# First batch's keys loaded by groups, values loaded by heads into 96 partitions, in a polysketch attention + tanh-shrink kernel

## The chip, the cores and the metric

The kernel runs on one core of a Trainium2 chip. The time is device microseconds (us) of one execution. Before the change three timed runs gave 104.93, 105.68 and 105.86 us, a median of 105.68 us; the execution that was profiled took 104.86 us.

## The reference

Everything is float32. B = 4 batches, H = 4 heads, S = 1088 positions, D = 32, sketch rank r = 8; the second part sees 4 x 1088 = 4352 tokens of 128 features.

```python
def phi(x):                        # x: (B, H, S, D)
    a = einsum('rd,bhsd->bhsr', S1, x)
    b = einsum('rd,bhsd->bhsr', S2, x)
    return einsum('bhsi,bhsj->bhsij', a, b).reshape(..., 64)
q_p, k_p = phi(q), phi(k)
kv  = einsum('bhsf,bhsd->bhfd', k_p, v)      # sum over positions
z   = sum(k_p, axis=2)
num = einsum('bhsf,bhfd->bhsd', q_p, kv)
den = einsum('bhsf,bhf->bhs', q_p, z) + 1e-6
x   = (num / den) as (B*S, H*D) = (4352, 128)
h   = x @ w_in                               # w_in: (128, 2048)
out = (h - tanh(h)) @ w_out                  # w_out: (2048, 128)
```

Since h @ w_out = x @ (w_in @ w_out), the kernel computes `x @ (w_in @ w_out)` from a folded 128x128 matrix and adds `tanh(-h) @ w_out`.

## The kernel before, in words

**Layout.** A head's 1088 positions stand as 32 rows (j) of 34 consecutive positions (c). Keys and queries lie with head and j on the 128 partitions. Positions are cut into 9 tiles t; a tile holds 4 groups g of 32 rows. With c = 9g + t the values `vx` lie with (g, j) on 128 partitions and head, t, d behind each other; the last group has 7 tiles instead of 9.

**Attention, first batch.** `load_keys` brings `kraw`, `load_rows` the queries, `load_v` the values. DVE turns the keys by 32x32 blocks (`kT`, L595), PE projects them on the sketches (`kproj`, L604), DVE turns the result back (`kab`, L612). Two things follow. (1) `gram` (L620) sums the products of the two sketches of the keys; `zm` (L625), `ufold` (L629) and `uw` (L632) make from it a column block of `w4`, with which PE projects the queries (`qproj`, L774); DVE turns the result (`qab`, L782), computes the denominators (`dm`, `den`, `rden`, `qa`: L801 to L810) and the query products `qp` (L685). (2) The key products `wk` (L652, on POOL and DVE) are multiplied with the values on PE (`tiles`, L665), copied (`kvs`, L671), folded (L674) and copied again (`kvb`, L678). Both meet: PE turns `qp` (`qt0`, L700), ACT copies it (`qpB`, L707), PE multiplies it with `kvb` (`num0`, L716), and a copy gives the tokens `xT` in bf16 (L722). The copy `ka` (L641) puts one factor of `wk` into PSUM for DVE.

**The second part.** Tokens go in ten windows of 256 or 512. For each window and each of 16 hidden blocks `jb`, PE computes h (`L1`, L952), ACT its tanh (L956), PE the product with `w_out` (`L2`, L973). `casts` makes bf16 copies of the weights, `linear_turn` turns `w_in` (L886, L891) and `wfold` (L898) makes the folded matrix. The first window needs the tokens of tiles 0 and 1 of the first batch. Batches 1 to 3 do the same attention in larger pieces between the windows' matmuls. While PE has nothing to do at the start, matmuls on zeros (`fill`, L531 and L532) are put into its stream.

**What sets the order.** Each engine has its own stream, and each instruction stands where the table `ORDER` puts it: operation numbers by engine, written out. `PLACES` names the engine of operations that can run on more than one. A planner in the source (`schedule`) places the fills and the waits by cost estimates; on the chip an engine takes its instructions in this order and stands at the first whose data is missing. SP issues nearly all transfers, on one queue, also in the order of the table; a load of a later batch waits until few enough bytes are outstanding (`gated`).

**Order at the start of before.** SP: keys in three pieces, queries 0 to 511, four loads of values, two slices of `w_in`, the rest of the queries, two slices of `w_in`, four of `w_out`, then batch 1. DVE: `kT` in two pieces, `kab` for tiles 0-4, `qT` (which waits for the queries), `kab` for tiles 5-8, `qT`, `wk` 5, `zm`, `wk` 6, `uw`, `wk` 7 and 8, `qab`. PE, from `qproj`: all nine tiles of `tiles` in one stretch (it waits for the value loads, all on one semaphore), the fold, `qt0` of tiles 0 and 1 with two `turn`s between, `qt0` of tiles 2 and 3, three `num0`, a `turn`, and the first `L1`.

The loads of values, keys and the loop of the first products are in these functions:

Of the kernel before, what the change touches and what calls it, by code (L numbers as in the profile page):

```python
# [30 lines left out]
COLD = 6800  # L31
EARLY = 5000
CHUNK = 256
HEAD = 56
# [19 lines left out]
    ),  # L54
    "scalar": (
# [4 lines left out]
    ),  # L60
    "vector": (
# [5 lines left out]
    ),  # L67
    "gpsimd": (
        "4 15 17 16 2 3 25 5 20 19 21 77 75 18 76 102 103 107 104 24 106 146 148 23 238 237 22 243 247 360 359 361 370 366 502 "
        "503 504 509 513 "  # L70
    ),
    "sync": (
# [7 lines left out]
PLACES = {"qpB0.2": "scalar", "w_inT0": "scalar", "x0.2": "scalar", "cast_out1": "scalar", "qpB0.4": "scalar", "qpB0.6":  # L80
          "scalar", "x0.4": "scalar", "kvs3": "scalar", "w_inT1": "vector", "x0.1": "vector", "w_inT2":
          "vector", "x0.8": "vector", "kvw1": "vector", "kvs2": "vector", "cast_in3": "gpsimd", "cast_out2":
          "gpsimd"}
# [22 lines left out]
class Program:  # L106
# [13 lines left out]
    def op(self, eng, cost, fn, r=(), w=(), prio=0.0, sem=None, mode=None, name="", after=(), ni=2, two=False, alt=None):  # L120
# [5 lines left out]
        o.alt = alt  # L126
        for k in r:
# [17 lines left out]
        for k in r:  # L145
            if k not in w:
                self.readers.setdefault(k, []).append(o)
# [9 lines left out]
    def schedule(self):  # L157
# [21 lines left out]
        while left:  # L179
# [20 lines left out]
            if e == "tensor":  # L200
                if filling and o in self.fill_stops:
                    filling = False
                if filling and fills_from in order["vector"]:
                    free[e] = max(free[e], fills_from.at + fills_from.cost + 90, 990)
                    while True:
                        rate = 1.2 if free[e] < COLD else 2.4
                        wide = 512 if free[e] + 512 / rate + 60 <= o.at else 128
# [3 lines left out]
                        f = Op("tensor", long, self.filler[0 if wide == 512 else 2], 0, None, None, "fill")  # L211
# [12 lines left out]
                while passed // CHUNK > block:  # L224
                    block += 1
                    self.fetch.append((block, o.name, o.at, have[block] - o.at))
                    o.at = max(o.at, have[block])
                    have.append(o.at + (5800 if o.at < 24000 else 3500))
# [134 lines left out]
def bass_polysketch_attn__then__act_tanh_shrink_kernel(nc, q, k, v, S1, S2, moe_w_in, moe_w_out, out):  # L363
# [11 lines left out]
    def dve(n):  # L375
        return 75 + n / 0.96
# [58 lines left out]
    KG = 9 * 32  # L435

# [25 lines left out]
    def load_small():  # L462
        for i, src in enumerate((S1, S2)):
            o = load("scalar", 1024, ("s_raw",), "s", -1000, lambda e, i=i, src=src: e.dma_start(
                out=s_raw[8 * i:8 * i + 8, :], in_=src[:, :]), True)
            o.lag = 800 * i - 500
# [16 lines left out]
    def load_keys(prio):  # L483

        src = k[0].rearrange("h (j c) d -> (h j) (c d)", j=32)
        dst = kraw[0][:, :].rearrange("p (g f) -> p g f", f=KG)

        def runs(g0, g1, lo, hi):
            rows = src[:, KG * g0 + lo:KG * g0 + hi]
            rows = bass.AP(tensor=rows.tensor, offset=rows.offset, ap=[rows.ap[0], [KG, g1 - g0], rows.ap[1]])  # L490
            return lambda e: e.dma_start(out=dst[:, g0:g1, lo:hi], in_=rows)  # L491

        for x, (g0, g1, lo, hi) in enumerate(((0, 4, 0, 160), (0, 3, 160, 288), (3, 4, 160, 224))):
            size = 512 * (g1 - g0) * (hi - lo)
            o = load("sync", size, ("kraw0", min(x, 1)), f"k0{min(x, 1)}", prio, runs(g0, g1, lo, hi), x == 2, (350, 378, 100)[x])
            o.lag = (-200, 150, 150)[x]
            if x == 2:
                asked.append((o, size))

    def load_v(b, prio):  # L500
        i = b % 2
        src = v[b].rearrange("h (j c) d -> j h c d", j=32)
        for g in range(4):
            n = 9 if g < 3 else 7
            o = load("sync", 128 * 128 * n, ("vx", i), f"v{i}", prio, lambda e, g=g, n=n: e.dma_start(
                out=vx[i][32 * g:32 * g + 32, :, 0:n, :].rearrange("j h t d -> j h (t d)"),
                in_=src[:, :, 9 * g:9 * g + n, :].rearrange("j h t d -> j h (t d)")), True, 190 if b == 0 else 240)
            o.lag = 1500 if b == 1 else 0 if b else 300
        asked.append((o, 128 * 128 * 34))
# [19 lines left out]
    def constants():  # L529
        wzero = P.op("vector", 150, lambda e: e.memset(wz[:, :], 0.0), w=[("wz",)], prio=-2000, name="wz")  # L530
        P.filler = (lambda e: e.matmul(ps[:, FB, 0:512], wz[:, :], wz[:, None, :].to_broadcast([128, 4, 128]), start=True, stop=True), wzero,  # L531
                    lambda e: e.matmul(ps[:, FB, 0:128], wz[:, :], wz[:, :], start=True, stop=True))  # L532
# [26 lines left out]
    def sketch():  # L559
        def put(e):  # L560
            for h in range(H):
                e.matmul(ps[32 * h:32 * h + 32, 5, 0:32], s_raw[:, :],
                         ident[0:16, None, 0:16].to_broadcast([16, 2, 16]),
                         start=True, stop=True, tile_position=(0, 32 * h))
            for h in range(H):
                ins = e.matmul(ps[32 * h:32 * h + 32, 6, 64:96], e16[:, :, :].rearrange("p a b -> p (a b)")[:, 32 * h:32 * h + 32],
                               s_raw[:, :], start=True, stop=True, tile_position=(0, 32 * h))
            return ins

        P.op("tensor", 170, put, r=[("s_raw",), ("ident",), ("e16",)], w=[bank[5], bank[6]], prio=-3000, mode="32x32", name="psk", ni=32)  # L570
# [14 lines left out]
    def keys(b, T, kb, gb, gate=()):  # L585
# [3 lines left out]
        for x, (lo, hi) in enumerate(KCUT if b else KPART):  # L589
            if b:  # L590
                P.op("vector", dve(hi - lo), lambda e, lo=lo, hi=hi: e.transpose(  # L591
                    out=kT[:, lo:hi], in_=kraw[i][:, lo:hi]), r=cells("kraw", i, lo, min(hi, S)) + ([("kraw0", i, "z")] if x else []),
                    w=[("kT", x)], prio=T["kT"], after=gate, name=f"kT{b}{x}")
# [524 lines left out]
```

## Time and profile before

| what | value |
|---|---|
| timed runs, median of 3 | 105.68 us (104.93 to 105.86) |
| profiled execution, its own time | 104.86 us |
| span of that execution's trace | 102.6 us |
| outside the span | 2.26 us |
| PE busy | 96.7 us, 94% of the span |
| ACT busy | 79.2 us, 77% |
| DVE busy | 60.0 us, 58% |
| POOL busy | 34.1 us, 33% |
| first L1 matmul (L952) | 15.7 us after the span's start |
| bytes moved | 11.21 MB |

A busy PE is not a PE at its peak, since matmuls overlap in their pipeline: the sum of the single durations is larger than the time that passes. The view that says what sets the end is the chain of waits, which is followed back from the last instruction. Times below are from the start of the span unless they are durations.

### The profile page before, as it was taken

How to read it: one execution, taken by the hardware profiler on the slowest of the kernel's cores; microseconds unless marked ns; L12 is line 12 of the kernel's file. 1: busy time of each engine (PE TensorE's matmuls, PEld its weight loads, DVE VectorE, ACT ScalarE, POOL GpSimd, SP SyncE). 2: the span in 40 equal slices, each digit the busy share in tenths (PEclk: the TensorE clock that was granted, in tenths of full speed). 3: DMA queues.
4: the chain of work that ended last, by engine and by line, in shares of the span. 5: the costliest groups of instructions: out<-in, count | busy, mean ns of one | idle time of the engine just before them, and what ended most of it. 6: DMA issues, size and time to landing. Idle time of an engine off the chain costs nothing.

```text
span 102.6 us, 3008 instructions
## 1 busy us (share of the span) xinstructions
PE 96.7 (94%) x1278; PEld 52.2 (51%) x1278; DVE 60.0 (58%) x129; ACT 79.2 (77%) x110; POOL 34.1 (33%) x43
## 2 busy tenths in 40 slices
PE   6969989999999999999999999999999999999970
PEld 2336747884676543434555343644444434445760
DVE  0778975997999897699678437837840020020120
ACT  3431768978767956787998797999869999999970
POOL 5347345420956800973910079083000000000000
PEclk9999999999999999999999999999999999999999
DMA  2999999910079804870003544030013611016254
GB/s 46 292 216 309 388 382 270 205 30 6 13 170 235 264 12 135 205 228 0 6 0 58 112 85 93 8 47 0 0 19 55 92 26 19 0 27 98 45 80 93
DMA packets 24029, 11.21 MB, mean 109 GB/s; under 512 B 18000, under 2 KB 21200, under 8 KB 24016
## 3 DMA queue, kind: packets, MB, share of 16 engines
q1 hardware_dynamic: 23840, 10.95, 44.2%
q8 instruction: 10, 0.16, 0.7%
q10 hardware_dynamic: 176, 0.07, 0.2%
q14 instruction: 3, 0.02, 0.1%
HBM read 8.78 MB, written 2.23 MB: 107 GB/s over the span
## 4 chain that ended last, share of the span: by engine, by line
PE 86%; DVE 5%; DMA 4%; SPq 1%; issue 0%
PE ps L952 31%; PE ps L973 27%; PE ps L843 4%; DMA qraw<-in_q_dram 4%; PE ps L937 4%; PE ps L734 3%; PE ps L774 3%; PE ps L716 2%; PE ps L604 2%; PE ps L700 2%; PE ps L968 2%; DVE qp L685 2%; SPq L491 1%; PE ps L620 1%; PE ps L898 1%; PE ps L629 1%
## 5 line engine op out<-in xcount | busy, mean ns | idle before, releaser
L956 ACT ACTIVATE tt<-ps 128x1024 bf16<-128x1024 f32 (+1 forms) x70 | 66.2, 998 | 8.0 <-PE ps L952 7.7
L952 PE MATMUL ps<-xT,w_in 128*128 128x512 bf16 (+1 forms) x160 | 42.7, 351 | 0.0
L973 PE MATMUL ps<-tt,w_out 128*128 128x512 bf16 (+1 forms) x144 | 38.2, 356 | 0.0
L952 PEld LDWEIGHTS ps<-xT,w_in 128*128 128x128 bf16 x160 | 16.3, 115 | 14.7 <-ACT tt L956 3.7
L652 POOL TENSOR_TENSOR wk<-kab 128x768 f32<-128x768 f32 (+2 forms) x11 | 15.5, 1405 | 21.0 <-DVE kab L612 20.4
L973 PEld LDWEIGHTS ps<-tt,w_out 128*128 128x128 bf16 x144 | 14.1, 99 | 11.9 <-issue 0.9
L989 DVE STREAM_TRANSPOSE osb<-ps 128x512 f32<-128x512 f32 (+1 forms) x9 | 5.9, 657 | 20.5 <-PE ps L973 20.3
L820 POOL TENSOR_TENSOR qp<-qa,qab 128x768 f32<-128x768 f32 x6 | 10.6, 1768 | 7.2 <-DVE qa L810 6.9
L826 DVE STREAM_TRANSPOSE qpT<-qp 128x768 f32<-128x768 f32 x9 | 8.6, 964 | 3.0 <-POOL qp L820 3.0
L782 DVE STREAM_TRANSPOSE qab<-ps 128x576 f32<-128x576 f32 (+2 forms) x10 | 6.0, 642 | 2.0 <-PE ps L774 1.7
L531 PE MATMUL ps<-wz 128*128 128x512 bf16 x14 | 5.7, 510 | 1.0 <-DVE wz L530 1.0
L762 DVE STREAM_TRANSPOSE qT<-qraw 128x576 f32<-128x576 f32 (+2 forms) x9 | 5.9, 657 | 0.2
L612 DVE STREAM_TRANSPOSE kab<-ps 128x576 f32<-128x576 f32 (+2 forms) x5 | 3.3, 654 | 2.7 <-PE ps L604 2.7
L843 PE MATMUL ps<-qpT,kvw 32*32 32x288 f32 (+1 forms) x192 | 4.6, 399 | 0.0
L591 DVE STREAM_TRANSPOSE kT<-kraw 128x576 f32<-128x576 f32 x6 | 4.5, 743 | 0.0
L855 ACT CAST xT<-ps 128x256 bf16<-128x256 f32 (+2 forms) x6 | 2.2, 373 | 2.4 <-PE ps L843 2.4
L734 PEld LDWEIGHTS ps<-wk,vx 128*32 128x32 f32 x216 | 3.2, 110 | 1.0 <-issue 0.6
L734 PE MATMUL ps<-wk,vx 128*32 128x64 f32 x216 | 3.6, 220 | 0.0
L700 PE MATMUL ps<-ident,qp 128*128 128x128 f32 (+1 forms) x18 | 3.1, 280 | 0.6 <-DVE qp L685 0.6
L707 ACT COPY qpB<-ps 128x512 f32<-128x512 f32 (+1 forms) x5 | 2.5, 500 | 1.4 <-PE ps L700 1.3
L843 PEld LDWEIGHTS ps<-qpT,kvw 32*32 32x32 f32 x192 | 2.4, 103 | 2.1 <-DVE qpT L826 0.5
L774 PE MATMUL ps<-qT,w 32*32 32x288 f32 (+2 forms) x160 | 3.4, 365 | 0.0
(99 smaller groups left out, 92.5 us busy)
## 6 DMA issues: line engine op xcount, KB each, us to landing
vx<-in_v_dram SPq DMA_DIRECT2D x12, 144.0 KB, 4.3
qraw<-in_q_dram SPq DMA_DIRECT2D x4, 288.0 KB, 5.2
qraw<-in_q_dram SPq DMA_DIRECT2D x4, 256.0 KB, 5.3
w_in_f<-in_moe_w_in_dram SPq DMA_DIRECT2D x4, 256.0 KB, 5.4
w_out_f<-in_moe_w_out_dram SPq DMA_DIRECT2D x4, 256.0 KB, 7.8
out_dram<-osb SPq DMA_DIRECT2D x16, 64.0 KB, 2.0
kraw<-in_k_dram SPq DMA_DIRECT2D x3, 288.0 KB, 4.4
kraw<-in_k_dram SPq DMA_DIRECT2D x3, 256.0 KB, 5.2
```

The costliest lines, as they stand in the source:

```text
L652: P.op(eng, dve(cols) if eng == "vector" else pool2(cols), lambda e, t0=t0, t1=t1, ap=ap, m=m, ka0=ka0: e.tensor_tensor(out=wk[:, t0:t1, : ...
L734: ins = e.matmul(ps[32 * h:32 * h + 32, vb, 0:64], vx[i][:, h, t, :], wk[:, t, h, :, :], start=(t == 0), stop=(t == NT - 1), tile_position ...
L762: P.op("vector", dve(hi - lo), lambda e: e.transpose(out=qT[i][:, lo:hi], in_=qraw[i][:, lo:hi]), r=cells("qraw", i, lo, hi), w=cells("qT" ...
L774: ins = e.matmul(ps[32 * g:32 * g + 32, qb + h, 0:n], w4[i][32 * h:32 * h + 32, :], qT[i][32 * h:32 * h + 32, :].rearrange("p (t g j) -> p ...
L782: P.op("vector", dve(2 * n), lambda e, h=h: e.transpose(out=qab[:, t0:t1, h:h + 2, :].rearrange("p t h x -> p h t x"), in_=ps[:, qb + h:qb ...
L820: P.op(eng, dve(cols) if eng == "vector" else pool2(cols), lambda e, p0=p0, p1=p1, w=w: e.tensor_tensor(out=qp[:, p0:p1, :, :, :].rearrang ...
L826: P.op("vector", dve(cols), lambda e, p0=p0, p1=p1: e.transpose(out=qpT[:, p0:p1, :, :, :].rearrange("p t h y j -> p (t h y j)"), in_=qp[: ...
L843: ins = e.matmul(ps[32 * h:32 * h + 32, nb[g], 0:32 * n], kvw[i][32 * g:32 * g + 32, y, 32 * h:32 * h + 32], qpT[32 * g:32 * g + 32, t0:t0 ...
L952: P.op("tensor", pe(n), lambda e, jb=jb + y, y=y, hb=hb: e.matmul(hb[:, n * y:n * y + n], hidden(w_in, jb), xT[:, f0:f0 + n], start=True, ...
L956: P.op("scalar", act(q * n), lambda e, un=un, hb=hb, q=q: e.activation(out=tt[:, un, 0:q * n], in_=hb[:, 0:q * n], func=AF.Tanh, scale=-1. ...
L973: P.op("tensor", pe(n), lambda e, jb=jb, un=un, y=y: e.matmul(acc[:, 0:n], w_out[:, jb, :], tt[:, un, n * y:n * y + n], start=(not f0 and ...
L989: P.op("vector", dve(n), lambda e: e.transpose(out=osb[u][:, 0:n], in_=acc[:, 0:n]), r=[ka], w=[("osb", u)], prio=slot0, name=f"osb{w}")
```

## The change

Values: before, each batch has four loads, one for each group g, of 32 partitions x 4 heads x 288 (the last 224) numbers. After, each batch has five: one for each head, which fills partitions 0 to 95 (three groups of 32 rows) with 288 numbers each, and one for the last group of all heads (32 partitions x 4 heads x 224). Both sides of a load have three dimensions; the head load's DRAM side is written as 3 runs (step 288) of 32 rows of 288 numbers.

Keys of the first batch: before, three loads (positions 0-159 and 160-287 of each group, and a rest); after, one for each group, 288 (the last 224) numbers per partition. The transposes `kT`, the projection and `gram` are cut to fit: four transposes of 288 columns, `kproj` by two groups at a time, `gram` in two parts, all tiles' halves still put together before `kab`.

The key products of the first batch are now nine of 256 columns (before: POOL 256, 512, 512, DVE four of 256), on DVE (tiles 3, 8, 6) and POOL (4, 1, 5, 0, 2, then 7); `ka` is in two parts, and every product waits for its part. `tiles` is cut by tile in the order 0, 5, 1, 6, 2, 7, 3, 8, 4, with a `turn` behind the first two; it waits for the value loads at its first tile. Denominators and products of query tile 3 move to POOL. The first window's `L1` is cut in halves of 128 tokens. `x0.0` and `x0.1` are both on DVE. The e16 matmul of `sketch` stands by itself, behind `kproj`. A third width of fill exists (256), and the planner's constants, `ORDER` and `PLACES` are new throughout.

Order at the start of after. SP: keys g = 0, 3, 1, 2, values head 0, queries 0-511, one slice of `w_in`, values heads 1 to 3 and the last group, the other slices of `w_in` and `w_out` in turns with the rest of the queries, then batch 1. DVE: `kT` x4, `kab` x2, `qT`, `zm`, `wk` 3, `qT`, `uw`, `wk` 8 and 6, `qab`, the denominators, `qp` 0, 1, 2, `xT` x2. PE, from `qproj`: a fill, tiles 0 and 5, a fill, `turn`, the other tiles, `qt0` of tiles 0 and 1, the fold, `qt0` of tiles 2 and 3, three `num0`, then `L1` halves with the three other `turn`s and the second `qproj` between them.

```diff
 def load_keys(prio):
-        for x, (g0, g1, lo, hi) in enumerate(((0, 4, 0, 160), (0, 3, 160, 288), (3, 4, 160, 224))):
...
+        for g in range(4):
+            lo, hi = KG * g, min(KG * g + KG, S)
+            o = load("sync", size, ("kraw0", g), f"k0{g}", prio, lambda e, lo=lo, hi=hi: e.dma_start(
+                out=kraw[0][:, lo:hi], in_=src[:, lo:hi]), rate=280)
 def load_v(b, prio):
-        src = v[b].rearrange("h (j c) d -> j h c d", j=32)
-        for g in range(4):
-            n = 9 if g < 3 else 7
-            o = load("sync", 128 * 128 * n, ("vx", i), f"v{i}", prio, lambda e, g=g, n=n: e.dma_start(
-                out=vx[i][32 * g:32 * g + 32, :, 0:n, :].rearrange("j h t d -> j h (t d)"),
-                in_=src[:, :, 9 * g:9 * g + n, :].rearrange("j h t d -> j h (t d)")), True, 190 if b == 0 else 240)
+        rows = v[b].rearrange("h (j c) d -> h j (c d)", j=32)
+        (row,), last = {x[0] for x in rows.ap[1:2]}, v[b].rearrange("h (j c) d -> j h (c d)", j=32)
+        for h in range(H):
+            part = bass.AP(tensor=rows.tensor, offset=rows[h].offset, ap=[[KG, 3], [row, 32], [1, KG]])
+            o = load("sync", 384 * KG, ("vx", i), f"v{i}", prio, lambda e, part=part, h=h: e.dma_start(
+                out=vx[i][0:96, h, 0:9, :].rearrange("j t d -> j (t d)"), in_=part), True, 270)
+        o = load("sync", 128 * 128 * 7, ("vx", i), f"v{i}", prio, lambda e: e.dma_start(
+            out=vx[i][96:128, :, 0:7, :].rearrange("j h t d -> j h (t d)"), in_=last[:, :, 3 * KG:S]), True, 200 if b == 0 else 240)
 def key_products(b, T, split, pb=None):
+            for (e0, e1), kb in zip(KPART, pb):
+                P.op("scalar", act(32 * (e1 - e0)), lambda e, e0=e0, e1=e1, kb=kb: mover(e)(
+                    ps[:, kb, 32 * e0:32 * e1], kab[i][:, 0, e0:e1, :, :].rearrange("p t h x -> p (t h x)")),
+                    r=[("kab", i, t) for t in range(e0, e1)], w=[bank[kb]], prio=T["wk"], name=f"ka{b}.{e0}", alt=either(32 * (e1 - e0)))
+            for t, _, eng in split:
...
+                P.op(eng, both[eng], product, r=[("kab", i, t)], still=[bank[pb[t >= KPART[1][0]]]],
+                     w=[("wk", t)], prio=T["wk"], name=f"wk{b}.{t}", alt=both)
 def layers(w, f0, n, widths, hooks):
-                P.op("tensor", pe(n), lambda e, jb=jb + y, y=y, hb=hb: e.matmul(
+                for o, m in ((0, n),) if f0 else ((0, n // 2), (n // 2, n // 2)):
+                    P.op("tensor", pe(m), lambda e, jb=jb + y, y=y, hb=hb, o=o, m=m: e.matmul(
-    key_products(0, opening, [(0, 2, "gpsimd"), (2, 4, "gpsimd"), (4, 5, "gpsimd")] + [(t, t + 1, "vector") for t in range(5, 9)], 1)
+    key_products(0, opening, [(t, t + 1, "gpsimd" if t < 5 else "vector") for t in range(9)], (1, 2))
-    summed = values_first(opening, 2, 3, [(0, 2), (5, 7), (2, 4), (7, 9), (4, 5)])
+    summed = values_first(opening, 2, 3, [(t, t + 1) for t in SUMMED])
```

More of the change, by code (lines that the diff above doesn't have):

```diff
@@ L118, in __init__, with op @@
         self.fetch = []
-    def op(self, eng, cost, fn, r=(), w=(), prio=0.0, sem=None, mode=None, name="", after=(), ni=2, two=False, alt=None):
+    def op(self, eng, cost, fn, r=(), w=(), prio=0.0, sem=None, mode=None, name="", after=(), ni=2, two=False, alt=None, still=()):
         if alt and name in PLACES:
@@ L126, in op @@
         o.alt = alt
+        for k in still:
+            o.deps.update(self.writer.get(k, ()))
         for k in r:
@@ L144, in op @@
             self.readers[k] = []
-        for k in r:
+        for k in (*r, *still):
             if k not in w:
@@ L206, in schedule @@
                         rate = 1.2 if free[e] < COLD else 2.4
-                        wide = 512 if free[e] + 512 / rate + 60 <= o.at else 128
+                        wide = next((x for x in (512, 256) if free[e] + x / rate + 60 <= o.at), 128 if rate < 2 else 256)
                         long = wide / rate + (3 if rate > 2 else 0)
@@ L210, in schedule @@
                             break
-                        f = Op("tensor", long, self.filler[0 if wide == 512 else 2], 0, None, None, "fill")
+                        f = Op("tensor", long, self.filler[(512, None, 128, 256).index(wide)], 0, None, None, "fill")
                         f.at, f.end = free[e], free[e] + long
@@ L227, in schedule @@
                     o.at = max(o.at, have[block])
-                    have.append(o.at + (5800 if o.at < 24000 else 3500))
+                    have.append(o.at + (6200 if o.at < 24000 else 3500))
             if o.two and e == "vector":
@@ L485, in load_keys @@
         src = k[0].rearrange("h (j c) d -> (h j) (c d)", j=32)
[L486 to L491, printed above, removed]
-        for x, (g0, g1, lo, hi) in enumerate(((0, 4, 0, 160), (0, 3, 160, 288), (3, 4, 160, 224))):
[L494 to L498, printed above, removed]
+        for g in range(4):
+            lo, hi = KG * g, min(KG * g + KG, S)
+            size = 512 * (hi - lo)
+            o = load("sync", size, ("kraw0", g), f"k0{g}", prio, lambda e, lo=lo, hi=hi: e.dma_start(
+                out=kraw[0][:, lo:hi], in_=src[:, lo:hi]), rate=280)
+            o.lag = -650
@@ L509, in load_v @@
+        o.lag = 1500 if b == 1 else 0 if b else 300
         asked.append((o, 128 * 128 * 34))
@@ L647, in key_products @@
             m = 4 * (t1 - t0)
-            near = pb is not None and eng == "vector"
             ka0, keys = ap[:, 0, :, :], [("kab", i, t) for t in range(t0, t1)]
-            if near:
-                ka0, keys = ps[:, pb, 32 * (t0 - e0):32 * (t1 - e0)].rearrange("p (m x) -> p m x", x=R), keys + [bank[pb]]
             P.op(eng, dve(cols) if eng == "vector" else pool2(cols), lambda e, t0=t0, t1=t1, ap=ap, m=m, ka0=ka0: e.tensor_tensor(
@@ L655, in key_products @@
                 op=ALU.mult), r=keys, w=[("wk", t) for t in range(t0, t1)],
-                prio=T["wk"] + n * T["wkstep"], name=f"wk{b}.{t0}", two=not near)
+                prio=T["wk"] + n * T["wkstep"], name=f"wk{b}.{t0}", two=True, alt={"vector": dve(cols), "gpsimd": pool2(cols)})
     def values_first(T, vb, tb, tiled):
@@ L687, in products_first @@
             in1=qab[:, t, :, None, R:2 * R].to_broadcast([128, H, R, R]), op=ALU.mult),
-            r=[("qa", t), ("qab", t)] + ([bank[sb0]] if near is not None else []), w=[("qp", t)], prio=T["qp"], name=f"qp0.{t}", two=near is None)
+            r=[("qa", t), ("qab", t)] + ([bank[sb0]] if near is not None else []), w=[("qp", t)], prio=T["qp"], name=f"qp0.{t}", two=near is None,
+             alt={"vector": dve(256), "gpsimd": pool2(256)} if near is None else None)
     def numerators_first(T, groups, nb, xeng):
@@ L802, in denominators @@
             out=flat(dm)[:, :, 0:R], in0=flat(qab)[:, :, 0:R], in1=flat(qab)[:, :, 2 * R:3 * R], op=ALU.mult),
-            r=[("qab", t) for t in ts], w=[("dm", t) for t in ts], prio=T["den"], after=gate, name=f"dm{b}.{t0}", two=True)
+            r=[("qab", t) for t in ts], w=[("dm", t) for t in ts], prio=T["den"], after=gate, name=f"dm{b}.{t0}", two=True,
+             alt={"vector": dve(8 * m), "gpsimd": pool2(8 * m)})
         P.op("vector", dve(8 * m), lambda e: e.tensor_reduce(
@@ L812, in denominators @@
             r=[("qab", t) for t in ts] + [("rden", t) for t in ts], w=[("qa", t) for t in ts] + ([] if near is None else [bank[near]]),
-            prio=T["den"], name=f"qa{b}.{t0}", two=near is None)
+            prio=T["den"], name=f"qa{b}.{t0}", two=near is None,
+             alt={"vector": dve(8 * m), "gpsimd": pool2(8 * m)} if near is None else None)
         return {} if near is None else {t: spot[:, 4 * (t - t0):4 * (t - t0) + 4, :] for t in ts}
@@ L856, in numerators @@
                 xb[:, g, 0:late, :], ps[:, nb[g], 0:32 * late].rearrange("p (t j) -> p t j", j=32)),
-                r=[bank[nb[g]]], w=[("x", b, t, g) for t in range(late)], prio=T["x"], name=f"x{b}.{t0}.{g}")
+                r=[bank[nb[g]]], w=[("x", b, t, g) for t in range(late)], prio=T["x"], name=f"x{b}.{t0}.{g}",
+                alt=either(n) if g > 1 and b < B - 1 else None)
             if b == B - 1:
@@ L892, in linear_turn @@
             w_inT[:, 4 * x:4 * x + 4, :].rearrange("p j c -> p (j c)"), bv[:, 0:512]),
-            r=[bank[bk]], w=[("w_inT", x)], prio=T, name=f"w_inT{x}", alt=either(512))
+            r=[bank[bk]], w=[("w_inT", x)], prio=T, name=f"w_inT{x}", alt={"scalar": act(512), "vector": dve(256)})
     def linear_product(T, bk):
@@ L951, in layers @@
             for y in range(q):
-                P.op("tensor", pe(n), lambda e, jb=jb + y, y=y, hb=hb: e.matmul(
-                    hb[:, n * y:n * y + n], hidden(w_in, jb), xT[:, f0:f0 + n], start=True, stop=True),
-                    r=[("w_in", (jb + y) // 4)] + xs, w=[used[n * y // 512]], prio=s, name=f"L1.{w}.{jb + y}")
+                for o, m in ((0, n),) if f0 else ((0, n // 2), (n // 2, n // 2)):
+                    P.op("tensor", pe(m), lambda e, jb=jb + y, y=y, hb=hb, o=o, m=m: e.matmul(
+                        hb[:, n * y + o:n * y + o + m], hidden(w_in, jb), xT[:, f0 + o:f0 + o + m], start=True, stop=True),
+                        r=[("w_in", (jb + y) // 4)] + xs[len(xs) * o // n:len(xs) * (o + m) // n], w=[used[n * y // 512]], prio=s,
+                        name=f"L1.{w}.{jb + y}" + ("" if f0 else f".{o}"))
                 where.append((un, y))
```

100 lines of the change are left out of this document (57 added, 43 removed), and 60 rows, old and new, of tables (ORDER, PLACES).

## The prediction

> **What bounds the kernel now.** I read the page first, for the span and the shares, then the chain of waits in order of time, which says where time is lost, then the start of the trace in order of time.
>
> ```profile
> span 102.6 us, 3008 instructions
> PE 96.7 (94%) x1278; PEld 52.2 (51%) x1278; DVE 60.0 (58%) x129; ACT 79.2 (77%) x110; POOL 34.1 (33%) x43
> PE 86%; DVE 5%; DMA 4%; SPq 1%; issue 0%
> ```
>
> PE makes 86% of the chain; the rest is the opening. The chain's pieces (start, duration, what):
>
> ```profile
> 1.79 0.50 SPq L491
> 2.33 4.19 DMA qraw<-in_q_dram
> ...
> 9.68 0.79 DVE qab L782 x2
> ...
> 13.55 0.66 PE ps L700 x4
> 14.20 1.33 PE ps L716 x12
> 15.53 0.35 PE ps L886 x4
> ...
> 16.31 0.48 PE ps L774 x32
> ...
> 18.08 0.44 PE ps L973 x4
> ...
> 18.62 0.89 PE ps L898 x16
> ...
> 39.31 0.65 PE ps L604 x16
> ...
> 58.02 0.65 PE ps L604 x16
> ...
> 99.52 0.29 DVE olast L982
> ```
>
> From 13.55 to 99.52 the chain stays on PE. So the end is the time at which PE gets through the opening, plus a fixed amount of PE work. I measure both kernels at one point: the **end of `wfold`**, 18.62 + 0.89 = 19.51 in before. Up to there both have done the same work (twelve L1 of 256 tokens or their halves, four L2, all four `turn`s, the second `qproj`, three `num0`), and behind it the same remains. What moves this point moves the end.
>
> **What the value loads do today.** In the waits and in the order of time:
>
> ```profile
> PEld ps L665 <- DMA vx<-in_v_dram: 0.2, 1, 0.2
> ```
> ```profile
> 0.99 2.74 PE L531 MATMUL ps<-wz 128*128 128x512 bf16 x6 [0.99 <-DVE wz L530]
> ...
> 5.12 0.48 ACT L557 ACTIVATE s2blk<-ps,mask 128x32 f32<-128x32 f32 x2
> ...
> 5.91 0.52 DVE L612 STREAM_TRANSPOSE kab<-ps 128x320 f32<-128x320 f32 x1 [0.45 <-PE ps L604]
> ...
> 6.51 1.77 POOL L652 TENSOR_TENSOR wk<-kab 128x256 f32<-128x256 f32 x2 [2.64 <-DVE kab L612]
> ...
> 7.68 0.61 PE L531 MATMUL ps<-wz 128*128 128x512 bf16 x2
> ...
> 8.33 0.38 PE L629 MATMUL ps<-zm,s2blk 128*128 128x32 f32 x2
> ...
> 8.73 1.07 POOL L652 TENSOR_TENSOR wk<-kab 128x512 f32<-128x512 f32 x1
> ...
> 8.99 0.51 PE L774 MATMUL ps<-qT,w 32*32 32x128 f32 x32
> ...
> 9.43 1.22 PE L665 MATMUL ps<-wk,vx 128*32 128x64 f32 x72
> ...
> 10.71 0.27 ACT L671 COPY kvs<-ps 128x128 f32<-128x128 f32 x1 [2.69 <-PE ps L665]
> ...
> 11.03 0.49 PE L674 MATMUL ps<-ident,kvs 128*128 128x128 f32 x2
> ...
> 12.29 0.21 ACT L678 COPY kvb<-ps 64x64 f32<-64x64 f32 x1
> 12.52 0.79 ACT L707 COPY qpB<-ps 128x256 f32<-128x256 f32 x2
> ...
> 14.24 0.58 ACT L707 COPY qpB<-ps 128x512 f32<-128x512 f32 x1 [0.93 <-PE ps L700]
> ```
>
> PE waits 0.2 us for the values: they land at about 9.4, just in time. Their margin is nothing, so whatever changes their landing matters at once, because everything of PE stands behind `tiles` in one stream.
>
> **Part 1: the head loads.** The DRAM side of the new load has an outermost count of 3, its SBUF side 96. How does a load spread over the 16 DMA engines? The queue rows say (packets, MB, share):
>
> ```profile
> q1 hardware_dynamic: 23840, 10.95, 44.2%
> q10 hardware_dynamic: 176, 0.07, 0.2%
> ```
>
> SP's queue has 90 transfers, whose shapes hold 22,400 rows; 23,840 - 22,400 = 1440 = 90 x 16: one extra packet per engine used, 16 each. ACT's queue has 8 + 8 rows of S1 and S2 and 128 of the last output, 144; 176 - 144 = 32 = 16 + 8 + 8. The loads with an outermost count of 8 ran on **8 engines**, not 16. I infer that a transfer is dealt out by its outermost count, in equal shares. Shares that fit both 96 and 3 are three of 32 rows, so I take it that each head load runs on **three engines**, and the same three each time. That two sides disagree occurs nowhere in before, so this is inferred, not shown.
>
> [...]
>
> Price: what goes through one of the three, in order of issue, in KB (of 1024 bytes; sizes from the shapes). Keys 544/16 = 34; head 0 108/3 = 36; queries 256/16 = 16; one `w_in` slice 16; heads 1 to 3 108; last group 112/16 = 7. Sum 217, of it 144 of head loads. Rates from the stretches (PE, PEld, DVE, ACT, POOL busy, clock, DMA share, GB/s):
>
> ```profile
> 1.00:2.00 1.00, 1.00 (x3) 0.41 (x4) 0.00 (x0) 0.29 (x1) 0.70 (x4) 1.00 0.12 13
> 2.00:3.00 1.00, 1.00 (x4) 0.30 (x2) 0.44 (x5) 0.99 (x1) 0.68 (x3) 1.00 0.95 245
> 3.00:4.00 1.00, 0.94 (x4) 0.30 (x2) 0.66 (x6) 0.20 (x1) 0.70 (x4) 1.00 1.13 308
> ...
> 6.00:7.00 1.00, 0.51 (x8) 0.22 (x4) 0.88 (x3) 0.00 (x0) 0.49 (x1) 1.00 1.05 215
> ...
> 9.00:10.00 1.00, 1.00 (x73) 0.80 (x76) 0.92 (x3) 0.00 (x0) 0.80 (x1) 1.00 1.06 389
> ```
> ```profile
> kraw<-in_k_dram SPq DMA_DIRECT2D x1, 32.0 KB, 2.9
> ```
>
> Per engine: 308 GB/s (keys) is 18.8 KB/us, 389 (weights) 23.7, 215 (values, now) 13.1. Transfers begin at 2.0. The keys (557 kB; 13 + 245 + 308 = 566) are through at 4.0, and their last load, issued at 1.79, lands 2.9 later at 4.7: 0.7 from moved to landed. For the head loads' rate I take the middle of 18.8 and 23.7, 21.2, because three engines alone can't crowd each other as 16 do, and the rows (1152 bytes) lie between those of the keys (512 and 640) and the weights (2048). So: keys 34/18.8 = 1.8, queries and weights 32/23.7 = 1.35, last group 0.3, heads 144/21.2 = 6.8; **landing V** = 2.0 + 10.25 + 0.7 = **13.0**. Bounds: all at 23.7, 2.0 + 9.2 + 0.7 = 11.9; heads at 13.1, 2.0 + 3.45 + 11.0 + 0.7 = 17.2.
>
> From V on, on PE and ACT: `tiles` with the `turn` and a fill issue until V + 1.55 (1.22 + 0.35, less the pipeline's end, plus the fill); two `qt0` (half of 0.66 each) until + 2.2; the fold 0.3, until + 2.5; `qt0` of tiles 2, 3 until + 3.15. ACT meanwhile: `kvs` until + 2.0, two `qpB` 0.8, two `kvb` 0.2 each, until + 3.2; the wide `qpB` 0.6, until + 3.8. The third `num0` begins there and takes half of 1.33: first work of the second part at V + 4.45. Then to the end of `wfold`: 24 L1 halves at 0.056 (the 16 of L898, also 128 wide, take 0.89), 1.34; three `turn`s of 0.35, 1.05; `qproj` 0.48; L2 0.44; `wfold` 0.89: 4.2. Sum **V + 8.7** = 21.7, against 19.51: **+2.2 us**.
>
> Other data in the same engines: `w_in`, the rest of the queries and `w_out` follow with 133 KB, 5.6 us, so the last lands at V + 5.6; ACT copies a `w_out` slice behind the first two tanh, about V + 6 to 7, and `wfold` at V + 7.8 needs it: hidden. Batches 1 to 3 put 144 KB of values through these engines, and with keys, queries and output about 255 KB, 12 us, per batch; PE takes 18.7 us for one (58.02 - 39.31, the key projections of batches 2 and 3): hidden. Cost nothing below V = 14; beyond it up to 1 us.
>
> [...]
>
> **Part 2: keys, products, halves, placing.** All of this lies ahead of V, if V is late, and costs nothing. If it isn't late: the second `kab` no longer stands behind `qT` and the queries (6.52 by the chain). The first `kab` still comes at about 6.0 and ends at 6.5; ACT then makes `ka` (0.3) and four `s2blk` (0.48 for two), until 7.8; `ufold` starts at 7.9 instead of 8.33, and what follows keeps its distances: `qproj` 0.66 later at 8.55 instead of 8.99, `qab` at 9.3, ending at 10.1. POOL makes six products of 256 at about 0.65 (1.77 less 1.07 is 0.70 for one of 256; bounds 0.54, half of 1.07, and 0.70), from 6.9, with a wait of 0.2 for `ka` and 0.25 for a denominator: tile 7 is ready at 11.0 to 11.1, PE's last four tiles end at 11.6. That is what V + 1.55 is above: the same chain with 10.05 in place of V ends `wfold` at **18.75**, 0.75 ahead of before. So V hides up to 10.05 and decides from there; up to 10.8 it costs less than all else gains. The gain isn't larger because one `turn` (0.35) moves behind the first L1.
>
> The end of the kernel has the same instructions, with reordering between batches: nothing, within 0.5 either way, since the chain has no idle there.
>
> **Forecast.** +2.2 on 104.86 gives 107.1 for an execution like the profiled one. That one lay 0.8 below the median of 105.68; against the median it is **107.9 us**.
>
> **Rivals.** (a) *The head loads use all 16 engines.* The page shows no load with unlike sides, so this can be. For it: 96 partitions are a multiple of 16. Then the values land at about 9, POOL's products bind, and `wfold` ends at 18.75: -0.75, 104.9 us. This is not slower. It decides as soon as V is under 10.05. (b) *Three engines, at today's slow rate for values*, 13.1 KB/us: V = 17.2, +6.4; and 255 KB per batch takes up to 19 us where PE takes 18.7, so later keys come late too: about 112. Against it: 16 engines crowd 32 partitions today, three would not. (c) *Three engines but quick*, V = 11.9: +1.1, 106.8.
>
> **How the numbers follow.** 1% of 105.68 is 1.06, about what a measurement of this kernel can tell from no change. Forecast with (c) as its lower end, 0.70; (a) 0.22; (b) 0.08. (a) is a third faster by over 1% and otherwise the same. Of the forecast 0.05 falls within 1%. Faster 0.07, same 0.20, slower 0.73. The range leaves out half of (a) and (b): 104.9 to 110.5; the forecast's own is 106.6 to 110.
>
> **What would show it.** After, SP's queue has 95 transfers with 21,888 rows, 16 of them head loads: 23,200 packets if these use three engines, 23,408 if 16. PE would wait for `vx` at its first tile from about 9.4 to 13, and DVE and ACT idle with it; the GB/s of that stretch would fall far below 389. Against me: `tiles` near 9.4 and a first L1 near 14.5. The forecast is wrong if the sides are dealt otherwise, or if a wait later in the batches, which I price at nothing, takes over.

## The result, and the profile after

The changed kernel takes **112.83 us** (median of 4 runs, 112.64 to 113.1); the kernel before took 105.65 us beside it (4 runs). The ratio is **1.069, 95% interval 1.064 to 1.074**: 7.2 us slower, where 2.2 were forecast. The profiled execution took 112.74 us, 7.88 more than that of before. Of the 112.74 us, 1.74 lie outside the span, against 2.26 in before, so a difference between the two spans is 0.5 us above one between the times.

The page of after: span, busy time, granted clock in 40 slices, SP's queue (packets, MB, share), and the chain's shares.

```profile
span 111.0 us, 3023 instructions
PE 99.2 (89%) x1280; PEld 54.5 (49%) x1280; DVE 57.7 (52%) x125; ACT 79.0 (71%) x110; POOL 39.0 (35%) x52
PEclk9999555599999999999999999999999999999999
...
q1 hardware_dynamic: 23200, 10.95, 39.6%
...
PE 67%; DMA 15%; SPq 10%; DVE 2%; issue 1%; ACT 1%
```

PE's share of the chain fell from 86% to 67%; what came in its place are DMA and SP's issuing of loads. The 23,200 packets are the count given in the prediction for three engines per head load (23,408 for 16). And the clock stands at half in four slices, 11 to 22 us.

The waits of after (total, times, longest), and then its chain in order of time (start, duration):

```profile
PE ps L689 <- DMA vx<-in_v_dram: 5.4, 1, 5.4
```
```profile
6.80 8.66 DMA vx<-in_v_dram
...
15.60 0.65 PE ps L689 x16
...
25.63 0.89 PE ps L926 x16
...
37.22 7.94 DMA qraw<-in_q_dram
...
45.18 0.78 DVE qT L787
...
47.08 0.72 PE ps L606 x16
```

The values land at 6.80 + 8.66 = 15.46; before, they were there at about 9.4. The first `tiles` begin at 15.60, `wfold` (here L926) ends at 25.63 + 0.89 = **26.52** instead of 19.51. Behind that, the chain leaves PE a second time: the queries of batch 2 land at 45.16, and only then can its keys and queries be turned and projected (L606 at 47.08). Ahead of that load, SP has been issuing others without a pause since 30.84. In before the chain stayed on PE there.

The stretches of after (length; PE, PEld, DVE, ACT, POOL busy; clock; DMA share; GB/s):

```profile
7.00:8.00 1.00, 0.61 (x10) 0.11 (x2) 0.00 (x1) 0.85 (x6) 0.92 (x2) 1.00 0.32 98
...
11.00:12.00 1.00, 0.00 (x0) 0.00 (x0) 0.93 (x6) 0.00 (x0) 0.86 (x2) 0.71 1.03 307
12.00:13.00 1.00, 0.00 (x0) 0.00 (x0) 1.00 (x5) 0.00 (x0) 0.72 (x2) 0.50 1.05 287
...
21.00:22.00 1.00, 1.00 (x12) 0.87 (x12) 0.32 (x2) 0.98 (x2) 0.23 (x2) 0.67 0.21 72
```

From 7 to 8 only 0.32 of the 16 engines' time is used, that of 5.1 engines, and 98 GB/s move; an estimate from that: the few engines with head loads have a queue, most others have nothing. From 9 to 18 all 16 are at work again, with the loads that stand behind (shares of 0.91 and more). With 1.00 in the row before and 0.50 in the row behind, a clock of 0.71 from 11 to 12 puts its fall to half at 11.42, and 0.67 from 21 to 22 its return at 21.66. So it was at half for 10.24 us, six of them with PE at work.

### The profile page after: what moved, and what is told of

Its sections match the earlier page's. It is cut to its first block, busy times and chain, and to the rows that moved or that the text cites. A ratio compares the mean times of both kernels' runs of the same rounds, so it can differ in the third digit from the quotient of the medians.

```text
span 111.0 us, 3023 instructions
## 1 busy us (share of the span) xinstructions
PE 99.2 (89%) x1280; PEld 54.5 (49%) x1280; DVE 57.7 (52%) x125; ACT 79.0 (71%) x110; POOL 39.0 (35%) x52
## 3 DMA queue, kind: packets, MB, share of 16 engines
q1 hardware_dynamic: 23200, 10.95, 39.6%
HBM read 8.78 MB, written 2.23 MB: 99 GB/s over the span
## 4 chain that ended last, share of the span: by engine, by line
PE 67%; DMA 15%; SPq 10%; DVE 2%; issue 1%; ACT 1%
PE ps L982 24%; PE ps L1004 21%; DMA vx<-in_v_dram 8%; DMA qraw<-in_q_dram 7%; SPq L511 6%; PE ps L725 3%; PE ps L966 3%; PE ps L870 3%; PE ps L689 2%; PE ps L759 2%; PE ps L999 2%; PE ps L799 2%; SPq L488 2%; SPq L501 2%; PE ps L741 1%; PE ps L606 1%
## 5 line engine op out<-in xcount | busy, mean ns | idle before, releaser
L982 PE MATMUL ps<-xT,w_in 128*128 128x512 bf16 (+2 forms) x176 | 42.7, 334 | 0.0
L676 POOL TENSOR_TENSOR wk<-kab 128x768 f32<-128x768 f32 x7 | 11.2, 1598 | 17.5 <-DVE kab L624 17.2
L847 POOL TENSOR_TENSOR qp<-qa,qab 128x768 f32<-128x768 f32 x7 | 11.9, 1707 | 6.7 <-DVE qa L836 6.4
L689 PE MATMUL ps<-wk,vx 128*32 128x64 f32 x72 | 2.4, 313 | 5.4 <-DMA vx<-in_v_dram 5.4
L598 DVE STREAM_TRANSPOSE kT<-kraw 128x576 f32<-128x576 f32 (+1 forms) x10 | 6.1, 632 | 0.1
L747 DVE CAST xT<-ps 128x128 bf16<-128x128 f32 (+1 forms) x3 | 1.3, 425 | 8.5 <-PE ps L741 8.5
L689 PEld LDWEIGHTS ps<-wk,vx 128*32 128x32 f32 x72 | 1.9, 169 | 5.9 <-issue 5.9
L709 POOL TENSOR_TENSOR qp<-qa,qab 128x256 f32<-128x256 f32 x4 | 2.8, 700 | 5.4 <-DVE qa L836 5.2
L664 POOL TENSOR_TENSOR wk<-kab 128x256 f32<-128x256 f32 x6 | 3.8, 625 | 2.7 <-ACT ps L657 2.2
L606 PE MATMUL ps<-kT,psk 64*32 64x288 f32 (+2 forms) x80 | 3.2, 365 | 0.7 <-DVE xT L882 0.6
```

The lines of the kernel that those rows point to most:

```text
L676: P.op(eng, dve(cols) if eng == "vector" else pool2(cols), lambda e, t0=t0, t1=t1, ap=ap, m=m, ka0=ka0: e.tensor_tensor(out=wk[:, t0:t1, : ...
L689: ins = e.matmul(ps[32 * h:32 * h + 32, tb, 0:64], vx[0][:, h, t, :], wk[:, t, h, :, :], start=(t == tiled[0][0]), stop=(t == tiled[-1][1] ...
L847: P.op(eng, dve(cols) if eng == "vector" else pool2(cols), lambda e, p0=p0, p1=p1, w=w: e.tensor_tensor(out=qp[:, p0:p1, :, :, :].rearrang ...
L982: P.op("tensor", pe(m), lambda e, jb=jb + y, y=y, hb=hb, o=o, m=m: e.matmul(hb[:, n * y + o:n * y + o + m], hidden(w_in, jb), xT[:, f0 + o ...
```

## The experiments

Times are medians with the range of the runs; the kernel before ran beside them on the same chip (medians 105.3 to 105.44), and the ratios are to those runs. The experiments ran on three chips, so two of them are best compared by their ratios.

**Values by groups: is it the head loads at all?** The changed kernel with the form of the value loads alone undone: again 32 partitions at a time, in five loads at the same places of SP's queue.

```diff
-            part = bass.AP(tensor=rows.tensor, offset=rows[h].offset, ap=[[KG, 3], [row, 32], [1, KG]])
+            part = by_group[:, h0:h1, 9 * g:9 * g + 9, :].rearrange("j h t d -> j h (t d)")
...
-                out=vx[i][0:96, h, 0:9, :].rearrange("j t d -> j (t d)"), in_=part), True, 270)
+                out=vx[i][32 * g:32 * g + 32, h0:h1, 0:9, :].rearrange("j h t d -> j h (t d)"), in_=part), True, 270)
```

> The changed kernel with its values loaded by groups again (32 partitions each, five loads in the same places of the queue), so that no load has an outermost count of 3; nothing else is changed. Theory A (each head load runs on three of the 16 DMA engines because its source has 3 runs outermost, and this is the whole loss): the values land before the products are ready, the stall at the first tile is gone, 23,408 packets less what the other row counts make, and the time is that of the rest of the change, 104.9 us, between 104.2 and 105.7. Theory B (the loss lies in the new order, the placing on POOL and the keys): the time stays near 112.8. Theory C (a destination of 96 partitions is slow in itself): 104.9 as by A, so this run doesn't part A from C.

Measured: 105.5 us (105.36 to 105.9, 12 runs), ratio 1.0016, interval 0.9991 to 1.0041. All of the loss goes with the form of these loads. With the values by groups, all other parts of the change together make no difference that can be measured. Its chain shows why they don't gain the 0.75 us of the prediction's Part 2:

```profile
6.48 0.53 DVE kab L625
...
11.07 0.33 POOL dm L827
...
11.47 0.64 POOL wk L665
...
12.15 0.65 PE ps L690 x32
...
19.04 0.89 PE ps L927 x16
...
38.59 0.99 PE ps L983 x4
...
39.79 0.65 PE ps L607 x16
```

POOL's last product ends at 12.11, where the prediction had 11.0 to 11.1; PE's last four tiles begin there, at 12.15, and `wfold` (L927) ends at 19.93, 0.4 behind before, not 0.75 ahead. (What lies outside the span is 1.78 us here and 2.26 in before; if that difference lies ahead of the span, `wfold` ends at the same time in both.) From 28.66 to 37.00 the chain runs over DVE and POOL, which in before it does not, and then through PE at 38 to 40; no load is in it there.

**Three forms of the source: 96 rows, 3 x 32, 6 x 16, of rows that lie behind each other.** They were to show whether the 96 partitions, the notation or the count of engines is slow. They load other rows of the values than the change does, so their output is not that of the reference.

```diff
-            part = bass.AP(tensor=rows.tensor, offset=rows[h].offset, ap=[[KG, 3], [row, 32], [1, KG]])
+            part = bass.AP(tensor=rows.tensor, offset=rows[0].offset, ap=[[row, 96], [1, KG]])
or
+            part = bass.AP(tensor=rows.tensor, offset=rows[0].offset, ap=[[32 * row, 3], [row, 32], [1, KG]])
or
+            part = bass.AP(tensor=rows.tensor, offset=rows[0].offset, ap=[[16 * row, 6], [row, 16], [1, KG]])
```

> The changed kernel; each head load writes to the same 96 partitions, but its source is one run of 96 rows (dimensions 96 x 288), other rows of the values than wanted, so the output isn't the reference's. Theory A: 96 outermost on both sides spreads over 16 engines; 23,408 packets; no stall at the first tile; 104.9 us, 104.2 to 105.7. Theory B: near 112.8. Theory C (96 partitions as destination are slow): near 112.8.

> As the run with 96 rows, with the very same addresses read and written, but the source is written as 3 times 32 rows (3 x 32 x 288); the output isn't the reference's. Theory A: three engines again, 23,200 packets, the values land at about 15.5 us of the span and the time is 112.8, 112 to 113.5. Theory C and a theory in which the addresses in DRAM matter (rows 1152 bytes apart): the same time as the run with 96 rows, whatever that is.

> The same addresses once more, the source written as 6 times 16 rows (6 x 16 x 288); the output isn't the reference's. Theory A: six engines, 21,888 + 79 x 16 + 16 x 6 = 23,248 packets; the four head loads bring 72 KB to an engine instead of 144, which at the rate that the changed kernel's landing at 15.46 gives (144 KB in 9.3 us) is 4.65 us less: landing at 10.8, no half clock, about 105.7 us, 105 to 106.5. Theory C: as the run with 96 rows.

Measured: 108.46 (105.63 to 108.94), 106.35 (105.85 to 107.34) and 107.06 (105.62 and 108.5). All three have 23,408 packets. The second and third miss what was expected of them (23,200 and 23,248): 3 x 32 and 6 x 16 rows that lie behind each other are one run of 96 rows, and by the packets all three ran as such, with 16 engines. They are taken as one kernel here; why its runs scatter from 105.62 to 108.94 was not settled. What remains is that 96 partitions filled by 16 engines are not slow by themselves: even the slowest run stays 3.9 us under the changed kernel.

**Six and 16 engines with strides that can't be joined.** The same number of bytes and rows, the same partitions and the strides of 288 and 1,088 elements as in the change; only the counts differ. These too load other rows of the values, which overlap in part.

```diff
-            part = bass.AP(tensor=rows.tensor, offset=rows[h].offset, ap=[[KG, 3], [row, 32], [1, KG]])
+            part = bass.AP(tensor=rows.tensor, offset=rows[h].offset, ap=[[KG, 6], [row, 16], [1, KG]])
or
+            part = bass.AP(tensor=rows.tensor, offset=rows[h].offset, ap=[[KG, 16], [row, 6], [1, KG]])
```

> The changed kernel with the head loads' source written as 6 by 16 rows instead of 3 by 32, with strides that can't be joined into one (288 and 1,088 elements), so that other rows of the values are loaded: the output is not the reference's, the bytes, the rows' length and the partitions are the same. Theory A (the outermost count of the source sets the number of engines): six engines, 23,248 packets; half of the bytes on each, so that the values land at about 10.8 instead of 15.46 and the tiles start at 11 to 12; 105.4 to 107.0. Rival C (the stride of 288 elements ahead of that of 1,088, by which neighbouring rows lie apart, is what is slow, not the number of engines): landing at 14.5 or later, 111.5 to 113.5.

> As the run with 6 by 16 rows, but 16 by 6 rows, with the same two strides; other rows of the values are loaded here too. Theory A: all 16 engines, 23,408 packets, tiles at 10.3 to 10.9, 105.0 to 106.5, as with the values by groups. Rival C (the strides): landing at 14.5 or later, 111.5 to 113.5.

Measured: 6 x 16 takes 106.32 us (105.8 to 107.88, 10 runs, ratio 1.008, 1.004 to 1.012), 16 x 6 takes 106.21 us (105.89 to 107.31, 7 runs, ratio 1.009, 1.005 to 1.013). The first on the page and in the chain:

```profile
q1 hardware_dynamic: 23248, 10.95, 40.6%
```
```profile
6.89 4.85 DMA vx<-in_v_dram
...
11.78 0.43 PE ps L689 x16
```

and the second on its page:

```profile
q1 hardware_dynamic: 23408, 10.95, 42.3%
```

So the dose goes as the number of engines: three land at 15.46, six at 11.74, with 16 PE waits for them for only 0.5 us at its first tile (5.4 with three); packets 23,200, 23,248 and 23,408 by 16 head loads with 3, 6 and 16 engines each. The strides are not the cause.

**The head loads alone, in the kernel before.** Every other engine keeps its stream.

```diff
 def load_v(b, prio):
-        for g in range(4):
-            n = 9 if g < 3 else 7
...
+        for h in range(H):
+            part = bass.AP(tensor=rows.tensor, offset=rows[h].offset, ap=[[KG, 3], [row, 32], [1, KG]])
```

> The kernel before with nothing changed but the form of its value loads: four loads of 96 partitions by heads and one of 32, in the places of the four loads by groups; every other engine's stream is as it was. Theory A (the head loads run on three engines of 16 and bring the values late, whatever the rest of the change is): 23,600 to 23,700 packets, the tiles start between 14.5 and 16, the time is 111 to 113.5, a ratio of 1.05 to 1.075. Rival D (the head loads are only slow together with the new order of the queue, keys by groups ahead of them): 105.7 to 107.5, a ratio under 1.02.

Measured: 116.32 us (115.8 to 116.96, 4 runs), ratio 1.104 (1.097 to 1.110), 23,696 packets. The rival falls: the old order with these loads is not better, it is 3.5 us worse than the changed kernel. My own number, 111 to 113.5, is missed too. The chain has the reason:

```profile
6.04 8.99 DMA vx<-in_v_dram
...
24.80 0.89 PE ps L901 x16
...
38.32 8.26 DMA qraw<-in_q_dram
46.61 0.71 DVE qT L765
```
```profile
46.00:48.00 2.00, 0.00 (x0) 0.00 (x0) 1.39 (x4) 0.34 (x1) 0.00 (x0) 1.00 0.77 200
48.00:50.00 2.00, 1.46 (x17) 0.40 (x18) 0.88 (x4) 0.00 (x0) 0.00 (x0) 0.60 0.80 214
```

The values land at 15.03 and `wfold` (L901) ends at 25.69, 6.2 behind before (7.0 in the changed kernel). But the batch-2 queries here find PE with no work left: from 46 to 48 it does nothing, and then the clock is low again (0.60 from 48 to 50). In the changed kernel PE is idle for only 0.64 us of these two. So with head loads the rest of the change is worth 3.5 us; which part of it shortens the second wait, no run separates.

**The clock.** PE has nothing to do from 10.2 to 15.6. Products of zeros in that gap keep it active; nothing else uses PE there.

```diff
 def project(e):
...
+            if (b, t0) == (0, 0):
+                for _ in range(22):
+                    P.filler[0](e)
```

> The changed kernel with 22 more products of zeros on PE (512 wide, 0.22 us each at the full clock) between its last work ahead of the values and the tiles; nothing else uses PE in that time. They end at about 14.8, so that PE rests for under 1 us instead of 5.4. Theory B (of the 11.0 us from the landing of the values to the end of wfold, 2.3 us are the half clock of rows 12 to 21): the tiles still start at 15.5, the granted clock is 0.9 or more in every row from 12 on, wfold ends at about 24.2 instead of 26.5, and the time is 110.0 to 111.0. Rival (the late values alone set the end, and the slower clock is hidden by the loads behind them, batch 2's queries above all): 112.4 to 113.0.

> As the run with 22 products of zeros in the wait for the values, with 17, since the 22 ran at the half clock at first and ended at 16.4, after the values. If only the half clock is at stake: they end at about 15.3, the tiles start at 15.5 to 15.7, wfold ends 8.7 to 9.0 us after that, at 24.3 to 24.6, and the time is 110.0 to 110.8. If the gain with 22 came from something else (an order of the loads, say), it stays at 110.9 or falls back towards 112.8.

Measured: with 22, 110.87 us (110.55 to 111.46, 4 runs); with 17, **110.21 us** (109.98 to 110.59, 4 runs), ratio 1.048 (1.043 to 1.052). The 22 end after the values are there (tiles at 16.39), as the clock had fallen, at 8.78, before they began, at 10.51; the 17 fit. The chain with 17, and the row in which its tiles begin, at the full clock:

```profile
15.82 0.43 PE ps L689 x16
...
23.77 0.89 PE ps L929 x16
```
```profile
15.00:16.00 1.00, 0.98 (x16) 0.37 (x18) 0.00 (x0) 0.00 (x0) 0.00 (x0) 1.00 1.04 349
```

From the first tile to the end of `wfold` it takes 24.66 - 15.82 = 8.84 us, against 26.52 - 15.60 = 10.92 in the changed kernel. The same instructions, 2.1 us: the half clock's price, in the profile; 2.6 in the medians, 2.3 by the ratios. The rival (the clock is hidden behind the loads) falls.

**Which batches?** Head loads in the first batch alone, and in batches 1 to 3 alone, values by groups in the others.

```diff
 def load_v(b, prio):
+        if b == 0:        # or: if b > 0
...
+        else:
+            by_group = v[b].rearrange("h (j c) d -> j h c d", j=32)
```

> The changed kernel with the values by heads in the first batch alone; batches 1 to 3 load theirs by groups, in the same places of SP's queue. Of the changed kernel's loss the opening holds 7.0 us (wfold ends at 26.52 instead of 19.51), and 1.4 more come by the end of its span. Theory A (the opening's loss is the first batch's head loads alone; the rest comes from the head loads of the later batches, behind which batch 2's queries wait on the same three engines): wfold ends at 26 to 27 and the time is 111.0 to 112.0. Rival E (the rest follows from the late opening by itself): 112.5 to 113.2, as the changed kernel.

> The changed kernel with the values by groups in the first batch and by heads in batches 1 to 3. Theory A: wfold ends at 19.5 to 20.3 as with groups throughout, batch 2's queries land 2 us or more later than there, PE waits for them, and the time is 106.5 to 109.5. Rival E (the later head loads are hidden, and the later loss followed from the opening): 105.2 to 106.0, as with groups throughout.

Measured: 111.45 us (110.96 to 111.73, 4 runs, ratio 1.059, 1.054 to 1.063) with the first alone, 106.92 us (105.87 to 107.43, 4 runs, ratio 1.018, 1.013 to 1.022) with the others alone. The first ends `wfold` where the changed kernel does; its chain:

```profile
6.81 8.74 DMA vx<-in_v_dram
...
25.65 0.89 PE ps L933 x16
...
41.08 1.52 POOL qp L854
...
46.41 0.65 PE ps L613 x16
```

and the chain with the later head loads alone:

```profile
18.98 0.89 PE ps L933 x16
...
30.53 7.80 DMA qraw<-in_q_dram
...
38.36 0.78 DVE qT L794
...
40.26 0.72 PE ps L613 x16
```

With the first alone the chain before batch 2's key projection (L613) runs through POOL's query products; with the later ones it runs through the queries' load, 7.80 us on its way, as in the changed kernel (7.94). Leaving the later head loads out of the changed kernel gains 112.83 - 111.45 = 1.4 us; putting them into the kernel by groups costs 106.92 - 105.5 = 1.4. By the ratios these are 1.1 and 1.7, so the size is rough, but both say that the later head loads cost something and that the opening isn't the whole. The trace shows less of it: the execution with the later head loads that was profiled was the quickest of its four, 105.87 us, and its L613 begins 0.47 us behind that of the kernel by groups (40.26 after 39.79). The opening is the other 111.45 - 105.5 = 5.9.

**A try at a gain.** By groups, with POOL's last product ahead of the denominators' product that stood in front of it.

```diff
 ORDER["gpsimd"]
-... 87 124 92 127 ...
+... 87 92 124 127 ...
```

> The changed kernel with the values by groups throughout, and on POOL the last product of the first batch's keys ahead of the second half of the denominators' product, which stood ahead of it (0.33 us). With groups alone the last tiles started at 12.15, behind that product. Theory (the earlier keys gain nothing because this product ends last): the last tiles start 0.3 us sooner, the first L1 product of the two up to as much, and the time is 105.1 to 105.5. Rival (qa, which waits for the denominators, is what sets the next step): the same as with groups, 105.4 to 105.7.

Measured: 106.28 us (105.44 to 107.82, 12 runs), ratio 1.008 (1.004 to 1.012). Nothing gained, rather 0.7 lost by the ratios against the groups' 1.0016. The denominators, later by a product, are needed too; that this is the reason is not shown. Which step it held up was not settled, and no version here beats the kernel before.

## Why the prediction was wrong in size

**Right.** The direction; the place (PE waits for `vx` at its first tile); the cause (three engines per head load, shown by packets and by the dose of 3, 6 and 16); that Part 2 lies ahead of the values and costs nothing while they are late. That the rest of the change saves 3.5 us once the head loads are in, by the kernel before with head loads, was not foreseen.

**The landing V: 13.0 forecast, 15.46 measured.** The step that failed is the rate of 21.2 KB/us for the head loads, argued from "three engines alone can't crowd each other"; no run shows such crowding. What they show: 217 KB on each of the three, between 2.0 and 15.46 - 0.7, is 217 / 12.76 = 17.0 KB/us over all; with six engines 73 + 72 = 145 KB until 11.74 - 0.7 is 16.0; in the kernel before with head loads 34 + 16 + 151 = 201 KB until 15.03 - 0.7 is 16.3. Few engines were no quicker one by one than the 18.8 of all 16 with keys, also where few were at work: from 7 to 8 the 98 GB/s at a share of 0.32 are an estimated 18.7 KB/us for each of the 5.1, and with 17 products of zeros 56 GB/s at 0.20 are 17.1. Whether the work of the others beside them, with shares of 0.91 and more from 9 to 18, slowed the three as well, no run separates. The upper bound of the prediction, 17.2 us, held. That the loads take longer to issue (below) has a part in this that no run separates. This is +2.5 us.

**From V to `wfold`: 8.7 forecast, 11.06 measured** (26.52 - 15.46). The step that failed is that the sum goes at the full clock: the clock was at half until 21.66, V + 6.2, and that cost 2.1 to 2.6. Where the clock stayed up, the first tile to `wfold` took 8.84, so the sum of the steps itself was right. This is +2.4.

These two and the 2.2 forecast are the 7.0 by which `wfold` is late in the span.

**"Batches 1 to 3: hidden": 1.4 us measured** in the medians by both experiments, 1.1 and 1.7 by the ratios. The step compared 12 us of transfers on an engine with 18.7 us of PE work per batch. That holds as a mean, but it leaves out the order: the queries of batch 2 are issued behind the head loads and land 7.94 us after that. (The 133 KB of other data in the opening are 130 by the shapes, 48 + 18 + 64; that changes nothing.)

**Part 2, if V isn't late: -0.75 forecast, nothing measured** (ratio 1.0016). The steps that failed are two starts on POOL and DVE: the first `kab` began at 6.48, not 6.0, and the last of POOL's products ended at 12.11, not 11.05. With that 1.06 added to 18.75 `wfold` would end at 19.8; it ended at 19.93. So 16 engines, rival (a), would have given no change, not a gain.

**The rivals.** (a), 16 engines, is refuted by 23,200 packets. (b), 13.1 KB/us, forecast about 112 and came nearest in time, but not for its reason: V was 15.46, not 17.2, and the rest was the clock. (c) is refuted by V.

## What to carry to other kernels

Before a load is rewritten into fewer, larger ones, look at the outermost counts of both sides: 96 partitions from a source written as 3 x 32 went over three engines of 16, and with one such load per head, values that had come just in time put PE 6 us behind. With the number of loads and rows known, the packet count of the queue tells how many engines were used (here 23,200 with three for each head load, 23,408 with 16), so it shows this before any time does. A late load can cost more than its lateness: here the clock fell to half during the wait, and that added 2.1 us after the data were there. Products of zeros on PE during the wait took it back (8.84 us from the first tile to the end of `wfold` instead of 10.92, and 110.21 us in all instead of 112.83).

## What the runs showed of the hardware that was not expected

**The low clock lasted 3.42, 6.82 and 10.24 us.** Worked out as above from rows with a clock between 0.5 and 1, it was low for 10.24 us in the changed kernel (11.42 to 21.66). In the kernel before with head loads it was low from 10.84 to 17.66:

```profile
10.00:11.00 1.00, 0.00 (x0) 0.00 (x0) 0.97 (x8) 0.00 (x0) 0.00 (x0) 0.92 1.00 289
...
17.00:18.00 1.00, 1.00 (x16) 0.57 (x7) 0.00 (x0) 0.71 (x2) 0.46 (x1) 0.67 0.91 344
```

which is 6.82, and with six engines from 12.38 to 15.80:

```profile
12.00:13.00 1.00, 1.00 (x33) 0.71 (x25) 1.00 (x3) 0.19 (x1) 0.87 (x2) 0.69 0.99 338
...
15.00:16.00 1.00, 1.00 (x8) 1.00 (x7) 0.00 (x0) 0.81 (x3) 0.74 (x3) 0.60 1.05 389
```

which is 3.42. These are three, two and one times 3.41. So in these three runs a stop of PE for a few us went with one, two or three times that length at the low clock, and a landing 0.4 us later (15.46 after 15.03) with 3.42 us more of it. How long a rest it takes is not shown: in the run with 22 products the clock fell, at 8.78, while PE had rested for no longer than 1.19 us:

```profile
8.72 0.56 PE L645 MATMUL ps<-zm,s2blk 128*128 128x32 f32 x2 [1.19 <-DVE zm L641]
```
```profile
8.00:9.00 1.00, 0.28 (x2) 0.31 (x3) 0.94 (x4) 0.16 (x1) 0.78 (x3) 0.89 0.87 179
9.00:10.00 1.00, 1.00 (x20) 0.38 (x35) 0.94 (x4) 0.46 (x1) 0.92 (x2) 0.50 0.88 257
```

How much work keeps it up, no run here tells.

**The head loads took longer to issue.** SP's stream in the changed kernel, and in the same kernel by groups:

```profile
4.50 2.25 SPq L511 DMA_DIRECT2D vx<-in_v_dram  x3
```
```profile
4.03 1.38 SPq L512 DMA_DIRECT2D vx<-in_v_dram  x3
```

0.75 us each instead of 0.46, with fewer packets; with 16 x 6 rows and 16 engines three took 1.85, 0.62 each; with 3 x 32 rows that lie behind each other, on the same 96 partitions, 1.37, 0.46 each. So the longer time goes with the form of the source, and not only with the number of engines.
